# A tuned attention-and-mixer kernel: staggered first batch, full-array scores from block-diagonal keys, two-chunk down products, spread sums

## Chip, cores, metric

One Trainium2 (trn2) chip, one NeuronCore. The metric is the device time of one execution in microseconds (us); a median of several executions is given. A profile of one execution comes with each kernel; its span is about two us shorter than the time of that execution.

## The reference

Linformer attention for 8 batches of 8 heads, then an MLP mixer over tokens and channels. Shapes are given in comments; inputs and output are fp32, the kernel works in bf16 with fp32 accumulation.

```python
# q, k, v: (8, 8, 1024, 64)   E, F: (64, 1024)
k_proj = einsum('ks,bhsd->bhkd', E, k)
v_proj = einsum('ks,bhsd->bhkd', F, v)
attn = softmax(q @ k_proj.T / sqrt(64))          # 1024 x 64 per head
x = (attn @ v_proj) -> (8, 1024, 512)
h = relu(x.T @ w_tok1) @ w_tok2                  # token mixing, 1024 -> 256 -> 1024
u = x + h.T
out = u + relu(u @ w_ch1) @ w_ch2                # channel mixing, 512 -> 1536 -> 512
```

## The kernel before

A batch has a *front* (loads, projections, scores, attention output, token mixing, and a transpose of `u`) and a *main* part (the up products with `w_ch1`, then the down products with `w_ch2` by a seven-product Strassen-Winograd scheme that needs four bf16 sums per block, made on VectorE). The front of batch b+1 is a generator whose steps are woven into the main part of batch b. Only the front of batch 0, called the startup here, has no main part beside it. Each engine works off its own instruction queue in order (in e1 below, the k and v loads wait behind the q load).

```python
def turn_q(b):                                   # query transposes, by DMA, two halves of four heads
    st["qT", b] = work.tile([P, H, 4, P], BF16, tag="qT", name="qT", bufs=1)
    for j in range(2):
        hs = slice(4 * j, 4 * j + 4)
        nc.sync.dma_start_transpose(out=st["qT", b][:, hs]..., in_=st["q", b][:, hs]...)
# ... cut
def score_step(b, h, kT, psf):                   # two concurrent 64x64 matmuls per head
    sco = psf("sco")
    for j in range(2):
        js = slice(j * D, (j + 1) * D)
        nc.tensor.matmul(sco[js, :], kT[js, h, :], st["qT", b][js, h]..., start=True, stop=True)
    at = work.tile([P, 512], BF16, tag="attnT", name="attnT", bufs=4)
    nc.scalar.activation(out=at, in_=sco, func=ACT.Exp, scale=scale)
    return at
# ... cut
def front(b):
    turn_q(b)
    yield
    # ... cut
    for j in range(4):                           # projections in four stretches
        kv_mm(b, kv_ps, slice(0, H), range(2 * j, 2 * j + 2))
        if j < 3:
            yield
    kv_vec(b, kv_ps, kprojs, slice(0, H))
    if b + 1 < B:                                # loads of the next batch: fp32 in HBM, bf16 in SBUF
        load_kv(b + 1, (0, H))
        load_q(b + 1, (0, H))
    yield
    kt_step(b, kprojs, kT, slice(0, H), front_ps)
    yield
    # ... cut: first score; then for each head the next score and ou_step; token mixing;
    #          u, and DMA transposes of u
```

The softmax here doesn't subtract the row's maximum and nothing guards it: scores larger than these inputs give would overflow.

## Time and profile before

| | us |
|---|---|
| median, first runs | 508.39 |
| span of the profile | 505.2 |
| startup, until up matmuls run without a break | 53.5 |
| batch 0 | 64.2 |
| batches 1 to 5, each | 57.2 |
| batch 6 | 56.9 |
| batch 7 (no front beside it) | 44.5 |

A batch is counted from its first up matmul, which follows the last down product of the batch before in the timeline of TensorE.

The page of the kernel before. Busy time of the engines (PE is TensorE's matmuls, PEld its weight loads, DVE is VectorE, ACT is ScalarE, POOL is GpSimd), and the granted TensorE clock in 40 slices, in tenths.

```profile
span 505.2 us, 8059 instructions
...
PE 458.3 (91%) x3139; PEld 273.2 (54%) x3160; DVE 321.3 (64%) x708; ACT 142.4 (28%) x259; POOL 96.2 (19%) x143
...
PEclk9996999899999999999999999999999999999999
```

The same by stretch, from the table of stretches of the kernel before. The columns are the stretch, its length, busy time and number of instructions of each engine, the granted clock, the share of busy DMA engines and GB/s.

```profile
core 0: us, PE busy (x) PEld busy (x) DVE busy (x) ACT busy (x) POOL busy (x), PEclk, DMA share, GB/s
0.00:53.50 53.50, 32.20 (x321) 24.22 (x322) 20.45 (x51) 14.92 (x29) 17.97 (x29) 0.90 1.16 193
53.50:117.80 64.30, 57.36 (x369) 32.80 (x370) 42.71 (x89) 17.32 (x31) 10.45 (x15) 0.95 0.63 118
232.30:289.50 57.20, 54.79 (x366) 31.79 (x368) 38.95 (x85) 16.62 (x30) 10.46 (x15) 1.00 0.68 130
...
460.90:505.20 44.30, 39.73 (x264) 25.52 (x262) 25.12 (x58) 10.49 (x19) 7.69 (x12) 1.00 0.16 60
```

After the startup TensorE is the limit, with about two us of holes in a batch. A busy TensorE is not one at its peak, so starts have to be read too. This is the timeline of TensorE in the score phase of one batch: start, duration, what, and in brackets the idle time before.

```profile
189.44 0.40 PE L179 MATMUL sco<-qT,kT 64*64 64x512 bf16 x2 [0.51 <-DVE kT L170]
189.78 1.90 PE L368 MATMUL g_ps<-uT,wc 128*128 128x512 bf16 x8
191.61 0.40 PE L179 MATMUL sco<-qT,kT 64*64 64x512 bf16 x2
191.95 0.40 PE L192 MATMUL ou_ps<-vbd,attnT 128*128 128x130 bf16 x4
192.18 1.03 PE L368 MATMUL g_ps<-uT,wc 128*128 128x512 bf16 x4
193.14 0.40 PE L179 MATMUL sco<-qT,kT 64*64 64x512 bf16 x2
```

Eight up matmuls take 1.73 us at full rate (0.86 for four), and 191.61 − 189.78 is 1.83: 0.1 us goes at the change into the 64x64 mode. The pair of scores, 0.213 us of columns, holds TensorE from 191.61 to 191.95, 0.34 us: 0.12 goes at the change back.

### The profile page before, as it was taken

The numbers are of one execution on the slowest core, as the hardware profiler recorded it, in microseconds if no ns is written. First come the engines' busy times: TensorE is split into PE (matmuls) and PEld (weight loads), VectorE is DVE, ScalarE is ACT, GpSimd is POOL, SyncE is SP. The second block draws the span as 40 slices with busy tenths as digits, with TensorE's granted clock in tenths as the row PEclk, the third lists the DMA queues.
The fourth block names the chain that finished last, engine by engine and source line by source line (L and its number), as shares of the span: only waits on it lengthen the run. The fifth ranks groups of instructions, "written<-read, shape, count | busy, mean of one in ns | idle before, by whom it ended". The sixth has DMA issues, their size and how long they took to land.

```text
span 505.2 us, 8059 instructions
## 1 busy us (share of the span) xinstructions
PE 458.3 (91%) x3139; PEld 273.2 (54%) x3160; DVE 321.3 (64%) x708; ACT 142.4 (28%) x259; POOL 96.2 (19%) x143
## 2 busy tenths in 40 slices
PE   2667997899989999999989999999989999999996
PEld 2455433575347733675347733576337833576475
DVE  2344468574686657774686747864786748774764
ACT  2223343102441135212441035212441035212410
POOL 7402020121203320131203310131203300131033
PEclk9996999899999999999999999999999999999999
DMA  9999929349681859368691759359591750044013
GB/s 177 204 205 184 158 48 202 74 112 182 107 145 49 192 101 197 56 135 182 103 156 42 179 116 191 59 131 198 87 169 43 168 125 1 1 127 126 1 43 127
DMA packets 97303, 61.88 MB, mean 122 GB/s; under 512 B 60400, under 2 KB 88560, under 8 KB 97264
## 3 DMA queue, kind: packets, MB, share of 16 engines
q0 software_dynamic: 29200, 29.36, 36.1%
q1 hardware_dynamic: 68064, 31.99, 27.0%
q8 instruction: 25, 0.41, 0.3%
q14 instruction: 14, 0.11, 0.1%
HBM read 59.24 MB, written 16.78 MB: 150 GB/s over the span
## 4 chain that ended last, share of the span: by engine, by line
PE 80%; DVE 12%; ACT 3%; DMA 2%; issue 1%; POOL 1%; POOLq 0%; ACTq 0%; DVEq 0%
PE g_ps L368 28%; PE be L419 13%; PE al L419 8%; PE ga L419 8%; PE h_ps L243 5%; PE u_ps L255 4%; PE ou_ps L192 4%; DVE x_sb L199 3%; PE sco L179 3%; PE kv_ps L159 3%; DMA q_sb<-in_q_dram 2%; DVE g L375 2%; PE h_ps L300 1%; PE u_ps L309 1%; DVE rdn L198 1%
## 5 line engine op out<-in xcount | busy, mean ns | idle before, releaser
L368 PE MATMUL g_ps<-uT,wc 128*128 128x512 bf16 x768 | 182.7, 380 | 0.0
L368 PEld LDWEIGHTS <-wc 128*128 128x128 bf16 x768 | 69.5, 98 | 80.5 <-issue 13.1
L377 ACT ACTIVATE g<-g_ps 128x512 bf16<-128x512 f32 x120 | 71.6, 597 | 137.7 <-PE g_ps L368 137.7
L419 PEld LDWEIGHTS <-S 128*128 128x128 bf16 x768 | 75.4, 98 | 25.1 <-issue 3.8
L375 DVE TENSOR_SCALAR g<-g_ps 128x512 bf16<-128x512 f32 x72 | 49.6, 689 | 56.1 <-PE g_ps L368 56.1
L444 POOL TENSOR_TENSOR W<-V,u_sb 128x256 f32<-128x256 f32 x32 | 21.4, 669 | 282.9 <-DVE V L437 282.9
L419 PEld LDWEIGHTS <-g 128*128 128x128 bf16 x576 | 56.3, 98 | 17.8
L419 PE MATMUL be<-dT,S 128*128 128x256 bf16 x384 | 53.0, 275 | 0.2 <-DVE V L442 0.2
L419 PE MATMUL al<-wc,g 128*128 128x256 bf16 x384 | 52.4, 273 | 0.6
L184 ACT ACTIVATE attnT<-sco 128x512 bf16<-128x512 f32 x64 | 37.6, 595 | 29.5 <-PE sco L179 29.5
L199 DVE TENSOR_TENSOR x_sb<-ou_ps,rdn 128x512 bf16<-128x512 f32 x64 | 44.2, 691 | 2.2
L432 ACT ACTIVATE K<-al 128x256 f32<-128x256 f32 x32 | 12.3, 384 | 118.2 <-PE al L419 85.1
L192 PE MATMUL ou_ps<-vbd,attnT 128*128 128x130 bf16 x256 | 26.9, 231 | 15.4 <-DVE x_sb L199 11.1
L259 DVE TENSOR_TENSOR u_sb<-u_ps,x_sb 128x512 bf16<-128x512 f32 x56 | 38.7, 691 | 0.5 <-PE u_ps L255 0.4
L192 PEld LDWEIGHTS <-attnT 128*128 128x128 bf16 x256 | 15.6, 101 | 33.9 <-issue 15.5
L179 PE MATMUL sco<-qT,kT 64*64 64x512 bf16 x128 | 26.4, 420 | 6.7 <-DVE kT L170 4.9
L198 DVE RECIPROCAL rdn<-ou_ps 128x8 f32<-128x8 f32 x64 | 13.1, 205 | 29.6 <-PE ou_ps L192 29.6
L243 PE MATMUL h_ps<-x_sb,wt 128*128 128x512 bf16 x98 | 30.3, 379 | 1.7 <-DVE x_sb L199 1.3
L255 PE MATMUL u_ps<-R_sb,wt 128*128 128x512 bf16 x105 | 31.8, 379 | 0.0
L419 PE MATMUL ga<-dT,S 128*128 128x256 bf16 x192 | 27.0, 277 | 3.8 <-DVE dT L466 3.3
L87 POOL DMA_DIRECT2D k_sb<-in_k_dram x11 | 9.4, 859 | 108.5 <-PE kv_ps L160 106.6
L437 DVE TENSOR_TENSOR V<-ga,K 128x256 f32<-128x256 f32 x32 | 13.5, 422 | 25.6 <-PE ga L419 24.5
(66 smaller groups left out, 459.7 us busy)
## 6 DMA issues: line engine op xcount, KB each, us to landing
out_dram<-o_sb SPq DMA_DIRECT2D x64, 256.0 KB, 2.3
k_sb<-in_k_dram POOLq DMA_DIRECT2D x7, 1024.0 KB, 9.6
v_sb<-in_v_dram POOLq DMA_DIRECT2D x7, 1024.0 KB, 13.8
q_sb<-in_q_dram POOLq DMA_DIRECT2D x7, 1024.0 KB, 17.9
wc<-in_moe_w_ch_dram POOLq DMA_DIRECT2D x4, 384.0 KB, 12.6
wc<-in_moe_w_ch_dram POOLq DMA_DIRECT2D x2, 768.0 KB, 17.4
k_sb<-in_k_dram POOLq DMA_DIRECT2D x4, 256.0 KB, 10.7
v_sb<-in_v_dram POOLq DMA_DIRECT2D x4, 256.0 KB, 10.4
```

The lines of the kernel that those rows point to most:

```text
L179: nc.tensor.matmul(sco[js, :], kT[js, h, :], st["qT", b][js, h].rearrange("d s p -> d (s p)"), start=True, stop=True,)
L184: nc.scalar.activation(out=at, in_=sco, func=ACT.Exp, scale=scale)
L192: nc.tensor.matmul(ou[:, s // 2, o : o + 2 * D1], at[:, s * P : (s + 1) * P], vbd[:, h, :], start=True, stop=True,)
L199: nc.vector.tensor_tensor(out=st["x", b][:, :, h * D : (h + 1) * D].rearrange("p (b k) d -> p b k d", b=2), in0=ov[:, :, :, 0:D], in1=rdn[ ...
L243: nc.tensor.matmul(h_ps, wt1[:, s, t * P : (t + 1) * P], st["x", b][:, s, :], start=(s == 0), stop=(s == SC - 1),)
L255: nc.tensor.matmul(u_ps, wt2[:, t, s::SC], st["R", b][:, t, :], start=(t == 0), stop=(t == TC - 1),)
L259: nc.vector.tensor_add(out=st["u", b][:, s, :], in0=u_ps, in1=st["x", b][:, s, :])
L368: nc.tensor.matmul(g_ps, wc1[:, dc, cc * P : (cc + 1) * P], uT[:, 4 * sh : 4 * sh + 4, dc, :], start=(dc == 0), stop=(dc == DMC - 1),)
L375: nc.vector.tensor_relu(out=o, in_=g_ps)
L377: nc.scalar.activation(out=o, in_=g_ps, func=ACT.Relu)
L419: nc.tensor.matmul(acc[:, 0:HF], l, r, start=start and c == 0, stop=c == CH - 1, skip_group_check=True,)
L444: nc.gpsimd.tensor_add(out=W15, in0=V15, in1=u[:, 4 + i, hi])
```

## The change

The intent was to fill TensorE. The startup's steps are sorted by the times at which their inputs are expected, so that the pairs of heads overlap; the first three quarters of four up blocks are done inside it. Keys are laid out block-diagonally, so that a score is one full-array matmul. All projections run in one stretch; keys and values leave PSUM by two engines; scores run two heads ahead of the attention output. All up relus go to ScalarE, the sums are spread one per up block, and down products treat two 128-row chunks at once, so that evictions and outputs are twice as large and half as many. Steps of a front carry costs instead of being counted. The load order of the start is changed as well. Cut to its core:

```diff
 def load_all(b):                      # new: was load_kv, load_q
+    load(b, "k", k)
+    load(b, "v", v)
+    load(b, "q", q)
@@ startup loads
-    k, v, q of each pair; wt1, wt2 after the first pair; wc1; wc2; batch 1 after the startup
+    q, k, v of each pair; wt1 after the second pair; wt2; wc1; batch 1; wc2
@@ score_step
-    for j in range(2):
-        js = slice(j * D, (j + 1) * D)
-        nc.tensor.matmul(sco[js, :], kT[js, h, :], st["qT", b][js, h]..., start=True, stop=True)
+    nc.tensor.matmul(sco, kbd[:, h, :], st["qT", b][:, h]..., start=True, stop=True)
@@ front(b)
     turn_q(b)
-    yield
-    for j in range(4):
-        kv_mm(b, kv_ps, slice(0, H), range(2 * j, 2 * j + 2))
-        if j < 3:
-            yield
-    kv_vec(b, kv_ps, kprojs, slice(0, H))
+    for si in range(SC):
+        k_mm(b, kv_ps, al, si, f)
+        v_mm(b, kv_ps, al, si, f)
+    k_out(b, kv_ps, al)
     if b + 1 < B:
-        load_kv(b + 1, (0, H))
-        load_q(b + 1, (0, H))
-    yield
+        load_all(b + 1)
+    yield 1.2
+    # ... cut: v_out, kt_step, score 0, score 1, then ou_step(h) and score h + 2
@@ up
-    if n % 8 in (1, 4, 6):
-        nc.vector.tensor_relu(out=o, in_=g_ps)
-    else:
-        nc.scalar.activation(out=o, in_=g_ps, func=ACT.Relu)
+    nc.scalar.activation(out=o, in_=st["g_ps", n], func=ACT.Relu)
+    up_sum(b)                         # one of four sums per block, was four in a row
@@ down: for j in range(2), two chunks in one PSUM bank; was for i in range(4)
-    nc.sync.dma_start(out=out_v[b, :, i, :], in_=o1)
+    nc.sync.dma_start(out=out_v[b, :, top, :], in_=o1)
@@ startup
-    attn(0); attn(hp), mix(hp - 1) for hp in 1..3; mix(3)
+    ev = steps with expected times; ev += fill; ev.sort(); run each
```

## The prediction

> **What bounds the kernel now.** Span 505.2 us (page), 3.2 us under the median. By the timeline: startup until the first full-width up matmul (53.5 us), batch 0 (64.2), six alike batches of 57.2, a last batch with no front beside it (44.3). TensorE is the limit after the startup: busy 54.8 of 57.2 us in the stretch 232.3 to 289.5 (table of stretches); VectorE 39.0, ScalarE 16.6.
>
> Columns per batch (up 96x512, down 168x256, projections 8 pairs x512, scores 8 pairs x512, attention output 32x130, token mixing 32x512, key transposes 8x64): 121,400. The Trainium skill, "TensorE: Matmul & The Clock Gate", section "Back-to-back issue gap", has N/2.4 + 2.5 ns; the trace agrees (four up matmuls 0.86 us, six down products 0.655). That is an estimate of 51.5 us, so 5.7 us per batch are lost, by the timeline of one batch:
> - Half-array stretches. The skill, "TensorEngine Tiling (Array Packing)", "Key Properties": changing the tiling mode drains the array. The trace agrees: about 0.1 us before and 0.12 after each. Projections take 4 stretches, scores 8, key transposes 1: about 2.8 us.
> - TensorE waits: key copy 0.40, key transpose copy 0.51, ScalarE 0.43, attention-output evictions on VectorE 0.76 and 0.16: 2.3 us. VectorE relus (691 ns) and four sums in a row (4 x 420 ns) stand before those evictions.
>
> **What the change does.**
> 1. Startup. Before, pairs run nearly one after the other; late query loads, key copies, exps and evictions (chain of waits) leave TensorE busy 32 of 53.5 us. After, all q, k, v land by 24.5 us (estimate: 1.25 us per 256 KB at the page's 205 GB/s, first at 8) and wt2 by 27. A chain of some 10 us for the last pair ends the startup near 35.5 us, with 2.6 us of up matmuls already done.
> 2. Full-array scores: same 216 ns, 8 half-array stretches fewer: -1.8 us per batch. One projection stretch for four: -0.65.
> 3. Relus off VectorE (9 x 691 ns per batch), sums spread, scores two ahead, keys copied from PSUM by two engines: most of the 2.3 us of waits go. I estimate VectorE and ScalarE near 90% busy in the score phase and leave 1 us.
> 4. Two-chunk down products: 24 evictions of 422 ns become 12 of 691, -1.8 us of VectorE, off the path. The bigger last output costs 1 us at the end. It also puts 1 MB just ahead of the query transposes, while scores come 6 us earlier in a batch: 0.3 us of wait.
> 5. wc2 now comes after batch 1's loads, at 56.5 us (10.5 MB at 205 GB/s). The weight differences on VectorE wait for it, with evictions queued behind: I leave 4 us of TensorE wait in batch 0, where those differences cost 3.3 before.
>
> **Sum.** 35.5 + batch 0 54.5 + 6 x 52.7 + last 44.6 = 451, + 3.2 = 454 us. Range 444 to 464. Faster 0.98, same 0.015, slower 0.005.
>
> **What will show it.** First full up block near 35 us; period 52 to 53.5; no gap around scores; VectorE waiting on wc2 near 52 to 57 us; TensorE waits for query transposes below 0.5 us per batch; last batch 44 to 45.
>
> **What would make it wrong.** In-order queues: startup steps are placed by assumed arrivals and stall together if loads land later. VectorE or ScalarE over 95% in the score phase would turn into waits on the attention-output bank (period above 54). Late query transposes could stall the first score 1 us or more per batch. wc2 may cost more than 4 us.

## More of the kernel before

Several chips were used. Every ratio is to runs of the kernel before on the same chip in the same rounds. The experiments ran on three chips, on which the kernel before had medians of 507.2 (e1 to e4), 509.3 (e5 to e8) and 508.1 us (e9, e10), so a difference of one or two us between experiments of different chips needs their ratios or their traces.

`q_sb`, `k_sb` and `v_sb` have one buffer each. So the k and v loads of batch b+1 start when the projections of batch b have read k and v, and the q load starts when the query transposes of batch b have read q.

Timeline of the queues that issue DMAs, first SyncE's, then GpSimd's, in the batch that begins at 232.1:

```profile
232.96 0.33 SPq L460 DMA_DIRECT2D out_dram<-o_sb  x1
233.40 5.38 SPq L102 DMA_TRANSPOSE qT<-q_sb  x2
```

```profile
243.73 0.92 POOL L87 DMA_DIRECT2D k_sb<-in_k_dram  x1 [12.23 <-PE kv_ps L160]
244.63 0.89 POOL L88 DMA_DIRECT2D v_sb<-in_v_dram  x1
```

The transposes are issued 1.3 us into the batch, and the trace has the second one landed at 241.1. The loads are issued at 243.7, after that. The two never meet, because the four projection stretches are spread over 11 us.

## The result and the profile after

| | before | after |
|---|---|---|
| median of the same rounds, us | 508.32 | 515.88 |
| span of the profile | 505.2 | 512.9 |
| startup | 53.5 | 42.1 |
| batch 0 | 64.2 | 55.3 |
| batches 1 to 5, each | 57.2 | 63.9, 64.2, 63.8, 62.8, 63.6 |
| batch 6 | 56.9 | 53.3 |
| batch 7 | 44.5 | 43.9 |

The ratio is 1.0145, with a 95% interval of 1.0122 to 1.0169: the kernel became 1.5% slower. Here and below, a ratio is the mean time of one kernel's runs over that of the other's of the same rounds, so it is not quite the ratio of the medians.

The page after, with the chain of waits (the work that ended last, followed back). The busy share of TensorE has fallen, and 18% of the span hangs on the query transposes. These were not among the causes named in the chain of before.

```profile
span 512.9 us, 7570 instructions
...
PE 444.9 (87%) x3060; PEld 279.3 (54%) x3096; DVE 260.6 (51%) x527; ACT 187.1 (36%) x333; POOL 88.6 (17%) x95
...
PEclk9999989996999969998899997999879999999999
...
PE 67%; DMA 19%; DVE 7%; SPq 3%; ACT 2%; issue 1%; DVEq 0%; ACTq 0%
PE g_ps L388 22%; DMA qT<-q_sb 18%; PE be L441 12%; PE al L441 8%; PE ga L441 8%; PE h_ps L244 5%; PE u_ps L256 4%; DVE x_sb L197 4%; SPq L95 3%; PE ou_ps L190 3%; PE sco L177 2%; PE kv_ps L145 1%; DVE rdn L196 1%; DMA EF_f<-in_F_dram 1%; PE h_ps L305 1%
```

The table of stretches after: startup, batch 0, batch 1, batch 6, batch 7.

```profile
core 0: us, PE busy (x) PEld busy (x) DVE busy (x) ACT busy (x) POOL busy (x), PEclk, DMA share, GB/s
0.00:42.10 42.10, 27.48 (x323) 20.97 (x326) 19.09 (x46) 16.98 (x35) 17.93 (x29) 1.00 1.15 193
42.10:97.40 55.30, 51.25 (x344) 32.11 (x348) 34.11 (x66) 22.11 (x39) 9.47 (x9) 0.97 0.96 167
97.40:161.30 63.90, 53.73 (x357) 33.12 (x360) 31.39 (x63) 22.05 (x39) 9.51 (x9) 0.92 0.67 116
415.70:469.10 53.40, 52.45 (x358) 32.69 (x362) 31.38 (x63) 21.94 (x39) 6.85 (x6) 1.00 0.34 79
469.10:512.90 43.80, 39.18 (x266) 25.71 (x263) 19.18 (x37) 15.52 (x26) 6.84 (x6) 1.00 0.18 73
```

Batches 1 and 6 run the same instructions on TensorE, VectorE and ScalarE and differ by 10.6 us. Batch 6 is the last one with a front, so there is no further batch to load: GpSimd issues six instructions in place of nine there, the three loads being gone. That is a comparison which the trace makes by itself. The timelines of batch 1 show how. SyncE's queue, GpSimd's queue, and TensorE:

```profile
98.39 0.33 SPq L491 DMA_DIRECT2D out_dram<-o  x1
98.82 12.51 SPq L95 DMA_TRANSPOSE qT<-q_sb  x2
```

```profile
101.44 0.91 POOL L82 DMA_DIRECT2D k_sb<-in_k_dram  x1 [7.76 <-PE kv_ps L150]
102.34 0.88 POOL L82 DMA_DIRECT2D v_sb<-in_v_dram  x1
```

```profile
111.05 1.03 PE L388 MATMUL g_ps<-uT,wc 128*128 128x512 bf16 x4
121.33 0.58 PE L177 MATMUL sco<-qT,kbd 128*128 128x512 bf16 x1 [9.25 <-DMA qT<-q_sb]
121.71 0.64 PE L190 MATMUL ou_ps<-vbd,attnT 128*128 128x130 bf16 x4
122.14 1.91 PE L388 MATMUL g_ps<-uT,wc 128*128 128x512 bf16 x4
```

The projections now end 4 us into the batch, so the k and v loads are issued at 101.4 and 102.3, while the second transpose is on its way. That transpose, issued at 102.22, lands at 121.28: 19.1 us, where it took 4.4 to 5.9 before. The fifth score, the first of the second half of the heads, waits 9.25 us for it. After the wait the granted clock is 0.5 until 124.3 (clock records of the trace), which is why four up matmuls take 1.91 us there in place of 1.03. The wait and the slow stretch together make the 10.6 us by which this batch exceeds batch 6. Batches 1 to 5 exceed it by 52 us in all (318.3 less five times 53.3). In these five batches seven scores wait for a transpose, 39.4 us together (in batches 3 and 5 the first transpose is late too, 9.5 and 8.6 us from issue to landing). After the waits TensorE works 26.9 us in all at a granted clock of 0.5. At half speed that loses some 13 us (an estimate), and the two together make about the 52.

### The profile page after: what moved, and what is told of

Read it like the earlier page. It is cut to its first block, busy times and chain, and to the rows that moved or that the text cites. A ratio compares the mean times of both kernels' runs of the same rounds, so it can differ in the third digit from the quotient of the medians.

```text
span 512.9 us, 7570 instructions
## 1 busy us (share of the span) xinstructions
PE 444.9 (87%) x3060; PEld 279.3 (54%) x3096; DVE 260.6 (51%) x527; ACT 187.1 (36%) x333; POOL 88.6 (17%) x95
## 4 chain that ended last, share of the span: by engine, by line
PE 67%; DMA 19%; DVE 7%; SPq 3%; ACT 2%; issue 1%; DVEq 0%; ACTq 0%
PE g_ps L388 22%; DMA qT<-q_sb 18%; PE be L441 12%; PE al L441 8%; PE ga L441 8%; PE h_ps L244 5%; PE u_ps L256 4%; DVE x_sb L197 4%; SPq L95 3%; PE ou_ps L190 3%; PE sco L177 2%; PE kv_ps L145 1%; DVE rdn L196 1%; DMA EF_f<-in_F_dram 1%; PE h_ps L305 1%
## 5 line engine op out<-in xcount | busy, mean ns | idle before, releaser
L388 PE MATMUL g_ps<-uT,wc 128*128 128x512 bf16 x768 | 198.5, 394 | 1.6 <-DVE uT L338 1.0
L420 ACT ACTIVATE g<-g_ps 128x512 bf16<-128x512 f32 x192 | 114.2, 597 | 132.7 <-PE g_ps L388 132.3
L388 PEld LDWEIGHTS <-wc 128*128 128x128 bf16 x768 | 74.4, 101 | 83.7 <-issue 16.0
L441 PEld LDWEIGHTS <-S 128*128 128x128 bf16 x768 | 75.3, 98 | 17.1 <-issue 0.3
L475 POOL TENSOR_TENSOR V<-V,u_sb 128x512 f32<-128x512 f32 x16 | 18.5, 1154 | 241.1 <-DVE V L470 241.1
L177 PE MATMUL sco<-qT,kbd 128*128 128x512 bf16 x48 | 20.8, 444 | 40.4 <-DMA qT<-q_sb 39.4
L441 PE MATMUL be<-dT,S 128*128 128x256 bf16 x384 | 48.8, 273 | 0.1
L466 ACT ACTIVATE K<-al 128x512 f32<-128x512 f32 x16 | 9.6, 597 | 92.3 <-PE al L441 92.3
L406 DVE TENSOR_TENSOR S<-g 128x512 bf16<-128x512 bf16 x48 | 20.2, 421 | 31.5 <-ACT g L420 31.5
L404 DVE TENSOR_TENSOR S<-g 128x512 bf16<-128x512 bf16 x48 | 20.2, 421 | 13.7 <-ACT g L420 13.5
L82 POOL DMA_DIRECT2D q_sb<-in_q_dram x11 | 9.2, 833 | 98.9 <-DMA qT<-q_sb 78.3
L441 PE MATMUL ga<-wc,S 128*128 128x256 bf16 x192 | 24.7, 273 | 0.0
## 6 DMA issues: line engine op xcount, KB each, us to landing
wc<-in_moe_w_ch_dram POOLq DMA_DIRECT2D x4, 384.0 KB, 13.9
```

Source lines behind the costliest of these rows:

```text
L177: nc.tensor.matmul(sco, kbd[:, h, :], st["qT", b][:, h].rearrange("d s p -> d (s p)"), start=True, stop=True,)
L388: nc.tensor.matmul(st["g_ps", n], wc1[:, dc, cc * P : (cc + 1) * P], st["uT", b][:, 4 * sh : 4 * sh + 4, dc, :], start=(dc == 0), stop=(dc ...
L404: nc.vector.tensor_sub(out=s3, in0=a11, in1=a21)
L406: nc.vector.tensor_add(out=s1, in0=a21, in1=a22)
L420: nc.scalar.activation(out=o, in_=st["g_ps", n], func=ACT.Relu)
L441: nc.tensor.matmul(acc[:, e * HF : (e + 1) * HF], l[:, lc + c, l0 + (2 * j + e) * P : l0 + (2 * j + e + 1) * P], r[:, rc + c, r0 : r0 + HF ...
```

## The experiments

The *turns* theory: the DMA engines serve the two queues packet by packet in turn, and a packet of a load carries 1 KB where one of a transpose carries 256 B, so that transposes beside a load get a fifth of the bytes. The *output* theory: the change puts 1 MB of outputs, in pieces of 512 KB, just ahead of the transposes in the same queue. The *schedule* theory: scores simply come too early for the transposes, whatever runs beside them. And for e3, a rival: loads use up the bandwidth or go first, whatever their packets.

### e1: loads in the order q, k, v

```diff
 def load_all(b):
+    load(b, "q", q)
     load(b, "k", k)
     load(b, "v", v)
-    load(b, "q", q)
```

> The changed kernel, with the next batch's loads issued as q, k, v instead of k, v, q. The q load must wait until the query transposes have read the tile, and the queue that issues loads is in order, so k and v wait with it: the transposes get the DMA engines to themselves. Turns theory (transposes are slow because their packets take turns with the larger packets of the k and v loads): second transpose lands 8 to 9 us after the first is issued, as in the batch without loads, no wait at the fifth score, batch period 53.3 to 54 us for all six, total 460 to 467 us. Output theory (the 1 MB of outputs just ahead in the same queue delays them): outputs stand as they did, so the wait of 9 us per batch and a total near 515 stay. Schedule theory (scores simply come too early for the transposes): also unchanged.

Measured: 463.32 us against 507.21, ratio 0.912 (0.910 to 0.915). All six batches take 53.25 to 53.27 us. The timelines of SyncE's and GpSimd's queues in batch 1:

```profile
100.30 5.31 SPq L95 DMA_TRANSPOSE qT<-q_sb  x2
```

```profile
108.65 0.92 POOL L82 DMA_DIRECT2D q_sb<-in_q_dram  x1 [13.49 <-DMA qT<-q_sb]
109.55 0.89 POOL L82 DMA_DIRECT2D k_sb<-in_k_dram  x1
110.42 0.91 POOL L82 DMA_DIRECT2D v_sb<-in_v_dram  x1
```

In the program no work was taken away and no wait removed; a wait was added to the k and v loads. In batches 1 to 6 of the trace no score waits for a transpose any more, and the clock stays at 1.00. The kernel is 52 us faster than with the other order. Outputs and scores stand where they stood, so neither can be the cause alone. The fifth score of batch 1, the one that waited 9.25 us, and the table of stretches for the repaired kernel, one of its batches:

```profile
113.39 0.38 PE L177 MATMUL sco<-qT,kbd 128*128 128x512 bf16 x1
```

```profile
core 0: us, PE busy (x) PEld busy (x) DVE busy (x) ACT busy (x) POOL busy (x), PEclk, DMA share, GB/s
...
205.40:258.60 53.20, 52.67 (x362) 32.56 (x360) 31.23 (x63) 21.94 (x39) 9.51 (x9) 1.00 0.69 139
```

### e2: outputs in pieces of 256 KB

```diff
-nc.sync.dma_start(out=out_v[b, :, top, :], in_=o1)
+for e in range(2):
+    nc.sync.dma_start(out=out_v[b, :, 2 * j + e, :], in_=o1[:, e, :])
 # and the same for o2
```

> The changed kernel, with each 512 KB output cut into two of 256 KB, the size of before; bytes and place unchanged otherwise. Turns theory: transposes still land 19 us after their issue, period 63 to 65, total within 1% of 515. Output theory: if large output descriptors are what blocks the transposes, the wait at the fifth score shrinks by at least half, total below 490.

Measured: 510.9 us, ratio to before 1.007 (1.003 to 1.010). Batches 1 to 5 take 61.7 to 64.0 us, and the second transpose 17.1 to 18.2. The output theory falls. The size of the pieces is worth about 1%, which was not looked into.

### e9: only k beside the transposes

```diff
 def load_all(b):
     load(b, "k", k)
-    load(b, "v", v)
     load(b, "q", q)
+    load(b, "v", v)
```

> The changed kernel with the loads in the order k, q, v: q waits for the transposes and v behind it, so k's 1 MB alone runs beside the transposes. A dose between none (second transpose 4.4 us from issue to landing) and k and v (17.6 to 19 us). Turns theory: a packet pair takes 106 ns on each of 16 engines (17 alone + 90 alone), so k's 1024 packets of 1 KB are through after about 7 us and the transpose ends soon after: 10 to 13 us from issue, landing at or just before the fifth score, wait under 1.5 us, period 53.3 to 54.8, total 462 to 470. If any load beside them blocks the transposes until all loads queued are through, it stays near 18.

Measured: 480.6 us, ratio 0.944 (0.940 to 0.948); batches 1 to 5 take 54.9 to 60.3 us, batch 6 takes 53.25. The dose is as expected: the second transpose takes 11.4 to 13.3 us. The total is not. The expectation took no account of the first transpose, which lands late here too in some batches (up to 10.2 us) and makes an earlier score wait. The largest wait is 4.2 us, and a stretch at a clock of 0.5 goes with four of the five waits. The dose in one table, the second transpose of batches 1 to 5 from issue to landing in each trace:

| load beside it | second transpose, us | kernel |
|---|---|---|
| none | 4.3 to 4.4 | e1 |
| k, 1 MB | 11.4 to 13.3 | e9 |
| k and v, 2 MB | 17.6 to 19.1 | after |

### e3: load packets of half the size

```diff
+def load_halves(b, name, src):
+    # ... cut: allocate the tile
+    for i in range(2):
+        xs = slice(i * 256, (i + 1) * 256)       # of 512 elements of a partition and head
+        nc.gpsimd.dma_start(out=st[name, b][:, :, xs], in_=src_v[:, :, xs])
 def load_all(b):
-    load(b, "k", k)
-    load(b, "v", v)
+    load_halves(b, "k", k)
+    load_halves(b, "v", v)
     load(b, "q", q)
```

> The changed kernel, k and v of later batches loaded in halves of the innermost run, so that a load packet writes 512 B instead of 1024 B; same bytes, same place in the order. Turns theory: packets alternate one for one, a pair now takes 17 + 45 ns on an engine instead of 17 + 90, so the second transpose lands about 10 us after the loads start instead of 16 to 18, the wait at the fifth score falls from 9 us to 0 to 3, period 54 to 57, total 465 to 485. Rival (the loads use up memory bandwidth or go first, whatever their packet size): landing and wait unchanged, total about 515.

Measured: 492.66 us, ratio 0.972 (0.967 to 0.976); batches 1 to 5 take 57.3 to 60.4 us, the second transpose 13.4 to 15.7 us. Both directions are as the turns theory says and not as the rival says, but the gain is 23 us (515.9 to 492.7), where 31 to 51 were expected. DMA packet records, counted by queue in stretches where both queues have work, or one alone (up to 32 of the packets counted in a cell have 4 B):

```
kernel, stretch in us     load packets (size)   transpose packets (size)   ns per packet on one engine
before, 236.5 to 239      none                  2251 (256 B)               17.8
before, 248.5 to 255      1279 (1024 B)         none                       81.3
after, 113 to 119.5       1002 (1024 B)         1013 (256 B)               103.8 and 102.7
e9, 108.5 to 111.5        457 (1024 B)          455 (256 B)                105.0 and 105.5
e3, 107 to 110.5          838 (512 B)           826 (256 B)                66.8 and 67.8
```

Where both have work, the two queues get the same number of packets within 1.5%. A pair takes about as long as the two packets alone, one after the other (17.8 + 81.3 = 99 against 104). So a transpose that moves 227 GB/s alone (0.568 MB in 2.5 us) moves 40 GB/s beside loads of 1 KB packets and 60 beside packets of 512 B. That is the turns theory as measured. The 67 ns of a pair in e3 are near the expected 62; what the expectation lacked is that in this trace the second transpose, issued at 103.2, moves almost nothing before 106.5, and both queues move little from 112.5 to 113.5. Like pauses stand in the trace of the changed kernel: the transpose issued at 102.2 moves almost nothing before 106, and both queues little from 110.5 to 111.5. In e1, without loads beside it, the second transpose of batch 3 is issued at 210.5 and moves from 211.75. What makes the pauses is open, and the turns theory does not explain them.

### e4: the kernel before, with its projections in one stretch

```diff
-for j in range(4):
-    kv_mm(b, kv_ps, slice(0, H), range(2 * j, 2 * j + 2))
-    if j < 3:
-        yield
+kv_mm(b, kv_ps, slice(0, H), range(SC))
 # ... cut: kv_vec and the loads stay behind it
+for j in range(4):
+    yield
```

> The kernel before, with all eight projection pairs in the first step of a front, so that the loads of the next batch start about 6 us earlier, beside the query transposes; scores stay at their places, some 19 us (first) and 22 us (fifth) into the batch. Turns theory: the second transpose now lands 18 to 20 us after its issue instead of about 8, and still no score waits more than 1 to 2 us, because scores come that late here; three half-array stretches fewer save 0.6 us per batch. Period 56 to 58.5, total 503 to 517. If slow transposes cost time by themselves, total rises by tens of us.

Measured: 497.26 us, ratio 0.979 (0.977 to 0.982), batches of 55.8 us. The experiment missed its purpose. In batch 3 of its trace the loads are issued at 235.9 and the second transpose lands at 236.5, so there is still no overlap to speak of, and transposes take 4.5 to 6.3 us. It says nothing about slow transposes. It does show a part of the change alone: each batch is 1.5 us shorter. Three half-array stretches fewer account for about 0.65 of that by the gaps above. The waits on the key copy (0.40 us) and on the key transpose copy (0.51, now 0.18) shrink too; in e4 the copies have several steps' time.

### e5, e6: two parts undone on the repaired kernel

Both ran on another chip than e1, so their batch lengths say more than their totals. e5 puts the 64x64 scores back, from the same keys:

```diff
-nc.tensor.matmul(sco, kbd[:, h, :], st["qT", b][:, h]..., start=True, stop=True)
+for j in range(2):
+    js = slice(j * D, (j + 1) * D)
+    nc.tensor.matmul(sco[js, :], kbd[js, h, js], st["qT", b][js, h]..., start=True, stop=True)
```

> On the repaired kernel (loads q, k, v: 463.3 us), the scores again as two concurrent 64x64 matmuls per head, from the same block-diagonal keys. If changing the tiling mode costs what the trace of before shows (about 0.1 us before and 0.12 us after each of 8 stretches), each batch with a front grows by 1.6 to 2.0 us, period 54.9 to 55.3, total 474 to 478. Rival (those gaps were evictions and dependencies that the new schedule hides): less than 4 us in total.

Measured: 469.81 us, ratio 0.923 (0.920 to 0.926), 6.5 more than e1; batches 2 to 6 take 54.43 us, 1.18 more. This lies between the two expectations. The timeline of TensorE shows why it is less than 1.8:

```profile
221.53 1.03 PE L390 MATMUL g_ps<-uT,wc 128*128 128x512 bf16 x4
222.49 0.40 PE L179 MATMUL sco<-qT,kbd 64*64 64x512 bf16 x2
222.82 0.40 PE L192 MATMUL ou_ps<-vbd,attnT 128*128 128x130 bf16 x4
223.06 1.03 PE L390 MATMUL g_ps<-uT,wc 128*128 128x512 bf16 x4
```

The changes of mode still cost 0.1 us going in (four up matmuls from 221.53 to 222.49 in place of 0.86) and 0.12 coming out (222.49 to 222.82 in place of 0.21). But three of the eight scores are followed by an attention output, and there TensorE has something to wait for anyway. In the same place of e1's timeline a score holds TensorE from 219.91 to 220.32:

```profile
219.91 0.38 PE L177 MATMUL sco<-qT,kbd 128*128 128x512 bf16 x1
220.32 0.39 PE L190 MATMUL ou_ps<-vbd,attnT 128*128 128x130 bf16 x4
```

That is 0.41 us, longer than in e5; the modelled end of the matmul hides the wait. So eight entries of 0.095, five exits of 0.12 and three times 0.08 less make 1.1 us, near the 1.18 measured.

e6 puts three of eight relus back on VectorE:

```diff
-nc.scalar.activation(out=o, in_=st["g_ps", n], func=ACT.Relu)
+if n % 8 in (1, 4, 6):
+    nc.vector.tensor_relu(out=o, in_=st["g_ps", n])
+else:
+    nc.scalar.activation(out=o, in_=st["g_ps", n], func=ACT.Relu)
```

> On the repaired kernel, three of eight up relus back on VectorE, as before. If VectorE relus ahead of evictions made TensorE wait, as the prediction says, waits on the attention-output bank return, 1 to 2 us per batch, period 54.3 to 55.3, total 470 to 478. Rival (VectorE at 31.5 of 53.4 us has room, the spread sums and the lookahead of two are enough): under 0.5 us per batch, total 462 to 467.

Measured: 467.01 us, 3.7 more than e1 (other chip, ratios 0.918 and 0.912 to before); batches take 53.72 us, 0.47 more. The table of stretches in the score phase, first of e1, then of e6, columns as above:

```profile
217.70:230.00 12.30, 11.81 (x71) 5.60 (x70) 9.72 (x25) 8.39 (x15) 0.41 (x1) 1.00 1.19 189
```

```profile
217.70:230.00 12.30, 11.43 (x68) 5.44 (x68) 11.50 (x28) 6.43 (x12) 0.93 (x2) 1.00 1.17 183
```

VectorE goes from 79% to 93% busy, and a batch is half a microsecond longer. The rival reading is the nearer one, at the very edge of its range (0.47 of 0.5 us per batch, 467.01 of 467).

### e7, e8, e10: the startup

e7 is e1 with no up matmuls inside the startup:

```diff
-PART = (0, 1, 2, 3)
+PART = ()
```

> On the repaired kernel, no up matmuls inside the startup (the list of prefilled blocks is empty). Backlog theory (the startup ends late because TensorE itself is still working off 128-column matmuls after the last load): taking 2.6 us of its work out ends the startup about 2.6 us earlier, the total stays within 1 us of 463. Chain theory (the startup ends late because of evictions and copies, TensorE has holes): the startup ends at the same time, the total rises by 2 to 2.6 us to 465 to 466.

Measured: 461.64 us, ratio 0.908 (0.905 to 0.910), 1.7 less than e1 (other chip) and the fastest kernel. The first up relu comes at 39.8 us in place of 43.2 in e1 and 41.9 after. The first projections start at 10.0 us in e7, 11.0 in e1 and 9.6 after, so counted from there it comes 2.4 to 2.5 us earlier than in both. That is nearly the 2.6 us of work taken out, as the backlog theory says, though the total fell by more than its 1 us. The traces differ in something else too: batch 0 of e1 has a TensorE wait of 2.0 us and then 3.4 us at a clock of 0.5, and that of e7 has neither. So prefilling up matmuls gained nothing that can be seen here, and that it costs time is not shown.

e8 is e1 with the startup's steps in the old order, the prefilled up matmuls last:

```diff
-tk, tv, tq = t_k[hp], t_v[hp], t_q[hp]
+tk, tv, tq = 100 * hp + 10, 100 * hp + 12, 100 * hp
-to = max(tv + 1.5, tk + 4.2)
-t1 = to + 2.6
-t2 = max(t1 + 1.7, t_w2 + 1.4 * hp)
+to, t1, t2 = 100 * hp + 50, 100 * hp + 160, 100 * hp + 170
-ev += fill
+ev += [(t + 1000, n, fn) for t, n, fn in fill]
```

> On the repaired kernel, the startup's steps in the old order (the attention of one pair whole, then the mixing of the pair before it), prefilled up matmuls last; load order and everything else as in the repaired kernel. If staggering is what shortened the startup from 53.5 to about 43 us, it returns to 49 to 53 us and the total rises by 7 to 12 us. If the load order and the two-engine copies did it, the total rises by less than 3 us.

Measured: 479.35 us, ratio 0.943 (0.940 to 0.945), 16 us more than e1 (other chip). Up matmuls run without a break from 55.8 us on, with none of them done by then. So without the stagger the other changes leave the startup 2 us longer than the 53.5 us of before, more than was expected. Part of this is the clock: the startup of e8's trace has 6.8 us at 0.5 (44.1 to 50.9) and that of before 10.2 us (41.7 to 52.0), while those of e1 and of the changed kernel have none. By halves that is up to 3.4 and 5.1 us (estimates). Whether the order of the steps brings the slow clock about was not tried.

e10 is e7 with the k and v projections of a pair interleaved, so that both column halves of the array work at once:

```diff
 for si in range(SC):
-    mm(b, kv_ps, hs, si, dict(start=(si == 0), stop=(si == SC - 1)))
-fin(b, kv_ps, hs)
+    f = dict(start=(si == 0), stop=(si == SC - 1))
+    k_mm(b, kv_ps, hs, si, f)
+    v_mm(b, kv_ps, hs, si, f)
+k_out(b, kv_ps, hs)
+v_out(b, kv_ps, hs)
 # and one step for both, at the time of v
```

> The repaired kernel without the prefilled up matmuls (461.6 us), with the startup's k and v projections interleaved, so that the two column halves of the array run at once. If the startup is bound by TensorE's backlog of 128-column matmuls, 64 matmuls of some 65 ns go beside others: the startup ends 1 to 2.5 us earlier, total 459 to 461. If latency from load to load binds it, keys come 1.2 us later per pair: total 462 to 464.

Measured: 464.62 us, ratio 0.913 (0.910 to 0.916), 3 us more than e7 (other chip). It does not decide between the two theories, because the clock differs: the table of stretches has a stretch at half clock in this startup (the last but two of its columns is the granted clock), and the traces of e1 and e7 have none there.

```profile
28.70:35.50 6.80, 5.67 (x53) 4.33 (x50) 2.82 (x8) 2.40 (x6) 3.39 (x4) 0.50 1.29 204
```

Half of 6.8 us is 3.4 us (an estimate), as much as the kernel lost. Keys come later in this order, and TensorE waits 0.7 us for each pair's key copy.

## Why the prediction was wrong, point by point

The prediction was 454 us with a range of 444 to 464, and 98% for faster. The kernel took 515.9.

| term | predicted, us | after | e1 |
|---|---|---|---|
| startup | 35.5 | 42.1 | 43.3 |
| batch 0 | 54.5 | 55.3 | 55.5 |
| batches 1 to 5 | 5 x 52.7 | 318.3 | 5 x 53.25 |
| batch 6 | 52.7 | 53.3 | 53.3 |
| batch 7 | 44.6 | 43.9 | 43.9 |

**The step that failed** is in point 4: it counted 1 MB of outputs ahead of the query transposes and allowed "0.3 us of wait". It measured 10.4 us per batch: 7.9 us of wait for the transposes, and the rest lost at half clock after the waits. That is 52 us in five batches, of the 62 us by which the span missed the predicted 451. The prediction saw that scores come 6 us earlier, and named late transposes as a risk, but looked only at what stands ahead of them in their own queue (e2: no effect worth naming). It did not ask what else the earlier projections set free: the k and v buffers, and with them 2 MB of loads in another queue, just when the transposes run. The rule was there to be looked up. The Trainium skill, "DMA: Bandwidth & Descriptors", section "Queues, rings and completion order", says that each DMA engine goes round-robin between the queues that have work, a whole packet at a time. Traces agree (1002 packets of loads against 1013 of transposes in the same 6.5 us). What follows from it is that a queue of small packets beside one of large packets gets a share of turns, not of bytes. With 18 and 81 ns per packet, both readable in the profile of before, the 512 KB of a transpose (2048 packets on 16 engines, 128 turns of 99 ns) need about 13 us beside loads (an estimate; in batch 1 the second transpose moved from 106 to 120.7). That would have been the estimate to make.

**Mode changes (point 2).** Right in kind, too large in size: 1.8 us predicted for full-array scores, 1.18 measured by undoing them (e5). The section on mode changes that the prediction cites agrees with the gaps in the traces.

**Waits (point 3).** The sum was right, the cause half wrong. One microsecond was left for waits, and e1's batches are 53.25 us where 52.7 was predicted. But the relus on VectorE, named first, cost only 0.47 us (e6). The projections in one stretch gave 1.5 us in the old kernel (e4), more than the 0.65 counted for the stretches. What the spread sums and the lookahead of two are worth was not tried alone.

**Startup (point 1).** The loads landed as predicted (last v at 24.7 us). The "chain of some 10 us" behind it was 17.4 us, TensorE being busy for 13.9 of them; without the prefilled matmuls it is still some 15 (e7). Without the staggering the startup's gain is lost (e8), with up to 3.4 us of the clock in that difference. Whether the excess is TensorE's backlog or waits of the in-order queues is open: e7 fits the first reading, e10 could not tell.

**Batch 0 and the weight differences (point 5).** wc2 landed at 58.8 us (56.5 predicted), the differences ran from 61.0 to 66.5, and TensorE waited 2.2 us behind them for an eviction. A stretch of 3.4 us at a clock of 0.5 followed, worth 1.7 us by halves (an estimate), so the 4 us left for this were nearly used. The length of batch 0 was predicted within 1 us. **The end (point 4).** The last batch is 0.7 us shorter than predicted.

So the arithmetic of TensorE was good to about 1% per batch; batch 6 of the changed kernel showed this without any further run, and e1 turned it into a kernel of 463.3 us. The forecast failed on one interaction of two DMA queues; all else that it missed, mostly the longer startup, comes to some 9 us (463.3 against 454).

## What to carry to other kernels

When a change moves work earlier, list the buffers that this frees and the transfers that then start, and look up in the trace what they will run beside; a DMA of small packets that is needed soon should not share its time with a large load. Where an in-order queue issues the loads, putting first the load that must wait for the urgent transfer holds back the others; here that cost nothing (53.25 us a batch, as in batch 6, which has no loads). A stage of the same trace that lacks one ingredient (here batch 6, the last with a front, which has nothing to load) is the cheapest experiment there is.

## What the Trainium skill lacked or had wrong

- "DMA: Bandwidth & Descriptors", "Queues, rings and completion order" states the round-robin by packets and gives a packet as some 9 to 17 descriptors. In the records of these traces 256 B transpose packets and load packets of 1024 or 512 B come in equal numbers (1013 to 1002, 826 to 838); whether such a record is a packet in the page's sense is not shown. The page does not draw the consequence: a DMA transpose falls from 227 to 40 GB/s beside a load of 1 KB packets, and to 60 beside 512 B packets.
- The same page's rules say nothing on the time of a DMA transpose beside ordinary DMAs. Here 512 KB took 4.4 us alone, 11.4 to 13.3 beside 1 MB of loads and 17.6 to 19.1 beside 2 MB.
- "TensorEngine Tiling (Array Packing)", "Key Properties" says that a change of tiling mode drains the array, without a figure. Here it is about 0.1 us going into 64x64 and 0.12 coming out.
- "TensorE: Matmul & The Clock Gate", "Why this matters for your kernels" warns of idle gaps over about 3 us. The traces agree for long gaps (clock 0.5 after a 9.25 us wait, until 124.3), but 3 us is no safe bound in them: 3.4 us at clock 0.5 came after waits of 2.0 (e1, batch 0), 2.2 (e9) and 2.4 us (changed kernel, batch 5), while waits of 2.4 to 3.0 us in e3 were not followed by any. And e10 shows 6.8 us at clock 0.5 with no idle gap of TensorE over 1.1 us after the startup's first projections. TensorE was busy 49% of the 3.4 us before; but the startup of before has such a stretch at 36% (from 30.1 us) and full clock, so what set it off is not shown.
